# Transposing the first pair's raw queries, and asking for norms two row chunks earlier in the first batch

## The chip, the cores and the metric

The kernel runs on one core of one Trainium2 chip. The metric is the device time of one execution in microseconds (us), as the median over runs. The core has five engines with a queue of instructions each: TensorE (PE; its weight loads are shown apart as PEld), VectorE (DVE), ScalarE (ACT), GpSimd (POOL) and SyncE (SP), which here only issues transfers. Each queue runs in order, and an instruction at its head that waits for another engine or for a transfer holds up all that stand behind it.

## The reference

```python
# attention: q, k, v are (8, 12, 448, 64); everything is float32
def rmsnorm(x, g):
    return x / np.sqrt(np.mean(x * x, axis=-1, keepdims=True) + 1e-06) * g
scores = 1/np.sqrt(64) * rmsnorm(q, g_q) @ rmsnorm(k, g_k).transpose(0, 1, 3, 2)
scores = scores - scores.max(axis=-1, keepdims=True)
attn = np.exp(scores); attn = attn / (attn.sum(axis=-1, keepdims=True) + 1e-09)
x = (attn @ v).transpose(0, 2, 1, 3).reshape(8, 448, 768)
# spectral mixing and feed-forward
u = x + np.real(np.fft.fft(np.fft.fft(x, axis=1), axis=2))
un = (u - u.mean(-1, keepdims=True)) / np.sqrt(u.var(-1, keepdims=True) + 1e-06)
out = u + np.maximum(un @ w_ch1, 0) @ w_ch2     # w_ch1 (768, 3072), w_ch2 (3072, 768)
```

The weights are given in double precision, and the kernel converts them on the chip.

## The kernel before

The eight batches go through two programs. `aux(b)` does the attention of batch b and its spectral mixing; `ffn(b)` does the feed-forward part. `aux(0)` runs alone at the start, then `ffn(b)` is merged with `aux(b+1)`, which are both written as generators that yield an estimated cost. The opening stage, `aux(0)`, ends with the first matmul of `ffn(0)` (`up`, L1033), and nearly all of the span lies behind it.

Attention works through the 12 heads in six pairs, and a pair's 448 rows in four chunks of 112. For a pair, `load_pair` (L225) issues four loads on SP into the tile `raw` (two buffers): q for two heads, then k for two heads. Behind the first pair it calls `load_gains` (L197), four more loads on SP. `norm_pair` (L265) takes the mean squares: ACT squares q and k at once, DVE sums over 64 columns and applies 1/D and epsilon, POOL raises to the power -0.5 (`ss`), and q and k are multiplied by it into `qkn`, on DVE for the first two pairs, on POOL for the rest of the first two batches. `transpose_pair` (L309) loads and norms a pair, yields, lets PE turn q (`QT`), yields, then k (`KD`; ACT multiplies it on its way out of PSUM by `gneg`, the negative product of both gains and the scale), and yields. In the first batch the turned q goes through a PSUM bank of the tag S, of which there are two.

`softmax_pair` (L366) goes over the chunks: PE makes the scores of two heads (in S banks for chunks 0 and 2, in ffn banks for 1 and 3 of the first batch), DVE takes the minimum of each row (the scores carry a minus sign; `mn`), ACT takes the Exp with scale -1 and that minimum as bias, and sums. `value_pair` (L484) turns the results (`pt`, `rem`) and multiplies by v (`av`) one pair later. `attention` (L530) interleaves three generators: a pair's chunks, the values of the pair before and, from the second chunk on, the norm and the transposes of the next pair.

The program is recorded in this order and a scheduler then places instructions on the queues, so the order on an engine isn't quite that of the code; buffers are handed out in the order of the code. Conversions of weights (`convert`, L777: two steps on ACT, four on DVE, one on ACT, one on DVE for each block) are fed into the opening stage by the count n of yields: 0.12 of a block for each, fifteen blocks in all. At n = 40 the DFT tables are loaded, and from n = 112 to 126 a step of `aux(1)` runs for each yield. `warm` (L1096) gives PE eight matmuls on zeros at the very start. Instructions of DVE, ACT and POOL in the attention are recorded by one helper and so carry its line, L116.

Of the kernel before, what the change touches and what calls it, by code (L numbers as in the profile page):

```python
# [92 lines left out]
def spectral_block(ctx, tc, q, k, v, g_q, g_k, w1, w2, d1, d2, out, nb=B):  # L93
# [103 lines left out]
    def load_gains():  # L197
        for half in (lo, hi):
            nc.sync.dma_start(gneg[half], g_q.rearrange("(d o) -> d o", o=1))
            nc.sync.dma_start(gtmp[half], g_k.rearrange("(d o) -> d o", o=1))  # L200
        V.scalar_tensor_tensor(
            out=gneg, in0=gneg, scalar=-(D**-0.5), in1=gtmp, op0=ALU.mult, op1=ALU.mult
        )
# [20 lines left out]

    def load_pair(b, p):  # L225
        if b >= nb or (b, p) in loaded:
            return
        at = ORDERS[b > 0][p]
        raw = sb.tile([C, 2, 2, NC, D], F32, tag="raw", name=f"raw{b}_{p}")
        for i, src in enumerate((q, k)):  # L230
            for h in range(2):
                nc.sync.dma_start(
                    raw[:, i, h],
                    src[b, 2 * at + h].rearrange("(c t) d -> t c d", c=NC),
                )
        if b + p == 0:
            load_gains()
        loaded[b, p] = raw
        if not plain(b, p):
            load_values(b, p)  # L240
# [23 lines left out]

    def norm_pair(b, p):  # L265
        raw = loaded.pop((b, p))
        qk = sb.tile([C, 2, NC, 2, D], F32, tag="qk", name=f"qkn{b}_{p}", bufs=1)
# [10 lines left out]
        for i in range(2):  # L278
            (G if 2 <= nth < NPAIR * 2 else V).tensor_tensor(
# [29 lines left out]
    def transpose_pair(b, p):  # L309
# [8 lines left out]
        if plain_s(b, p):  # L318
            T = []
            for i, tag in enumerate(("QT", "KD")):  # L320
                pt = bank(QK_BANKS[b > 0][i], f"qk{b}_{p}_{i}")
                for c in range(NC):
                    nc.tensor.transpose(
                        pt[:, c * C : (c + 1) * C],
                        qk[:, i, c].rearrange("t h d -> t (h d)"),
                        ident[:C, :C],
                    )
# [38 lines left out]
    def softmax_pair(b, p, Pc):  # L366
# [3 lines left out]
        for c in range(NC):  # L370
# [31 lines left out]
            for h, s_ in enumerate(banks):  # L402
                V.tensor_reduce(mn[:, h : h + 1], s_, axis=AX.X, op=ALU.min)
                freed[tag] = A.activation(
# [4 lines left out]
                    scale=-1.0,  # L409
# [120 lines left out]
    def attention(b, xT, EO):  # L530
# [3 lines left out]
        for p in range(NPAIR):  # L534
# [4 lines left out]
            ahead = transpose_pair(*next_pair(b, p))  # L539
            for i in range(4):  # L540
                yield next(rows)
                for _ in range(2):
                    yield next(values, 0)
                if i >= 1:
                    yield next(ahead, 0)
# [550 lines left out]
    def warm():  # L1096
# [4 lines left out]
        for _ in range(8):  # L1101
# [52 lines left out]
```

## Time and profile before

| | us |
|---|---|
| median of 3 runs | 2117.45 (2114.3 to 2120.1) |
| the profiled execution, its own time | 2118.55 |
| span of its trace | 2116.8 |
| first matmul of the feed-forward part | at 172.06 |

The mean clock granted to PE over the span is 0.987 of full. In the trace's tables, each row starts with the time from the span's start and the duration. A bracket at a row's end gives the time for which the engine had been idle before, and what released it. Busy times are of single engines and overlap each other. "x2" means that two instructions of the same kind were merged into a row, whose duration is that of both.

### The profile page before, as it was taken

Reading aid. Unit: us, or ns where it says so; the run is one execution under the profiler, and the core shown is the slowest. Engines: PE = TensorE matmul, PEld = TensorE weight load, DVE = VectorE, ACT = ScalarE, POOL = GpSimd, SP = SyncE. Lnnn points to the kernel's source line nnn. Section 1 sums busy time; section 2 is a strip of 40 time slices with the busy share of each in tenths; the row PEclk is TensorE's granted clock in tenths of the full one; section 3 lists DMA queues with packets and bytes.
Section 4 is the critical chain, followed back from the end, with each engine's and each line's share of the span. In section 5 each row is a group of like instructions: output and inputs, shape, how many; then the busy total and the mean of one; then the engine's idle time right before and its main releaser. Section 6 shows DMA issues by size and latency. Waiting matters only on the chain.

```text
span 2116.8 us, 31277 instructions
## 1 busy us (share of the span) xinstructions
PE 2069.4 (98%) x11288; PEld 1813.9 (86%) x11288; DVE 1510.5 (71%) x2882; ACT 1109.8 (52%) x2436; POOL 195.1 (9%) x109
## 2 busy tenths in 40 slices
PE   7879999999999999999999999999999999999999
PEld 3346777999999999999999999999999999998998
DVE  6788999877875778667885778758786678743122
ACT  6878886555534666256652566436662465422100
POOL 3321110000100110000110011001000001000000
PEclk8998999999999999999999999999999999999999
DMA  7565979776556745576565855567555764459664
GB/s 228 172 178 202 309 244 298 243 225 181 168 183 202 223 150 177 178 239 183 172 188 171 247 167 170 185 196 221 173 164 178 235 196 150 153 172 291 196 217 152
DMA packets 294494, 422.12 MB, mean 199 GB/s; under 512 B 182994, under 2 KB 221315, under 8 KB 294340
## 3 DMA queue, kind: packets, MB, share of 16 engines
q1 hardware_dynamic: 293572, 419.43, 64.5%
q8 instruction: 90, 1.47, 0.3%
q10 hardware_dynamic: 768, 0.69, 0.1%
q14 instruction: 64, 0.52, 0.1%
HBM read 360.27 MB, written 65.28 MB: 201 GB/s over the span
## 4 chain that ended last, share of the span: by engine, by line
PE 90%; DVE 3%; ACT 2%; DMA 2%; issue 1%; SPq 1%; POOL 0%; DVEq 0%; ACTq 0%; POOLq 0%
PE h L1033 33%; PE o L1054 32%; PE S L399 6%; PE av L519 4%; PE pt L507 4%; PE y L650 2%; PE S L392 1%; PE qk L343 1%; PE x L682 1%; PE oT L966 1%; PE av L453 1%; PE rem L488 1%; DMA u_dram<-u 1%; PE un L911 1%; PE pt L445 1%
## 5 line engine op out<-in xcount | busy, mean ns | idle before, releaser
L1054 PE MATMUL o<-hs,w 128*128 128x448 f32 x3420 | 772.6, 370 | 2.6 <-DMA w<-w 2.5
L1033 PE MATMUL h<-unT,w 128*128 128x448 f32 x3402 | 765.9, 369 | 1.1 <-ACT unT L116 0.9
L1054 PEld LDWEIGHTS o<-hs,w 128*128 128x128 f32 x3420 | 632.3, 188 | 58.4 <-issue 7.7
L1033 PEld LDWEIGHTS h<-unT,w 128*128 128x128 f32 x3402 | 627.7, 188 | 55.1 <-issue 4.1
L116 ACT ACTIVATE P<-S,mn 112x448 f32<-112x448 f32 x384 | 243.7, 638 | 187.7 <-DVE mn L116 183.3
L116 DVE TENSOR_REDUCE mn<-S 112x1 f32<-112x448 f32 x384 | 234.4, 618 | 50.4 <-PE S L399 35.8
L116 ACT ACTIVATE hs<-h 128x448 fp32r<-128x448 f32 x192 | 104.3, 543 | 296.5 <-PE h L1033 295.3
L116 POOL TENSOR_TENSOR ss<-ss,nhalf 112x16 f32<-112x16 f32 x48 | 146.5, 3052 | 1123.8 <-DVE ss L116 1123.8
L116 DVE SCALAR_TENSOR_TENSOR hs<-h,hs 128x448 fp32r<-128x448 f32 x192 | 119.3, 621 | 147.1 <-ACT hs L116 145.8
L116 DVE TENSOR_TENSOR acc<-o,acc 128x448 f32<-128x448 f32 x240 | 148.4, 620 | 89.9 <-PE o L1054 88.4
L116 ACT CAST T<-pt 128x448 fp32r<-128x448 f32 x216 | 113.4, 531 | 94.2 <-PE pt L507 92.1
L116 DVE TENSOR_TENSOR T<-pt,T 128x448 fp32r<-128x448 f32 x216 | 132.5, 620 | 36.8 <-ACT T L116 35.3
L519 PE MATMUL av<-T,vhl 128*128 128x448 f32 x432 | 153.3, 385 | 0.0
L116 DVE TENSOR_SCALAR P<-P,sm 112x448 f32<-112x448 f32 x312 | 129.3, 452 | 4.9
L507 PE MATMUL pt<-ident,P 112*128 112x112 f32 x864 | 121.7, 259 | 0.0
L507 PEld LDWEIGHTS pt<-ident,P 112*128 112x128 f32 x864 | 102.8, 140 | 16.5
L399 PE MATMUL S<-KD,QT 128*112 128x448 f32 x288 | 110.0, 382 | 0.0
L399 PE MATMUL S<-rounded,QT 128*112 128x448 f32 x288 | 105.5, 366 | 0.0
L519 PEld LDWEIGHTS av<-T,vhl 128*128 128x128 f32 x432 | 80.7, 188 | 6.8
L392 PE MATMUL S<-KD,QT 64*112 64x448 f32 x192 | 64.2, 647 | 14.3 <-ACT KD L116 5.7
L116 POOL TENSOR_TENSOR rstd<-st,nhalf 112x1 f32<-112x1 f32 (+2 forms) x32 | 20.4, 636 | 608.7 <-DVE st L116 604.5
L116 ACT ACTIVATION_READ_ACCUMULATOR P<-S,mn 112x1 f32 x384 | 76.4, 199 | 0.0
(147 smaller groups left out, 2420.2 us busy)
## 6 DMA issues: line engine op xcount, KB each, us to landing
w<-w SPq DMA_DIRECT2D x285, 512.0 KB
w<-w SPq DMA_DIRECT2D x189, 768.0 KB
dblw<-w SPq DMA_DIRECT2D x30, 512.0 KB
dblw<-w SPq DMA_DIRECT2D x15, 768.0 KB
raw<-q SPq DMA_DIRECT2D x96, 112.0 KB
raw<-k SPq DMA_DIRECT2D x96, 112.0 KB
v<-v SPq DMA_DIRECT2D x96, 96.0 KB
u_dram<-u SPq DMA_DIRECT2D x24, 336.0 KB
```

The costliest lines, as they stand in the source:

```text
L116: ins = emit(*args, **kwargs)
L343: nc.tensor.transpose(pt[:, c * C : (c + 1) * C], qk[:, i, c].rearrange("t h d -> t (h d)"), ident[:C, :C],)
L392: mm = nc.tensor.matmul(s_, QT[hs, cs], KD[hs], start=True, stop=True)
L399: nc.tensor.matmul(s_, QT[:, h, cs], K[:, h], start=step == 0, stop=step == 1)
L445: nc.tensor.transpose(pt[:, c * C : (c + 1) * C], piece, ident[:C, :C])
L453: mm = nc.tensor.matmul(av[a, :S], v_[:, j, h], T[h], start=j == 0, stop=False)
L488: nc.tensor.transpose(rem[:, c * C : (c + 1) * C], Pc[c][:, 384:512], ident[:C, :C])
L507: nc.tensor.transpose(pt[:, c * C : (c + 1) * C], Pc[c][:, 512 * h + j * 128 : 512 * h + (j + 1) * 128], ident[:C, :C],)
L519: nc.tensor.matmul(av[:, :S], lv, T[:, i], start=(j == 0 and i == 0), stop=False)
L650: nc.tensor.matmul(o, src[:, par, t0 : t0 + n], D1[:, ri, par, cols], start=i != 1, stop=i != 0,)
L1033: pace(nc.tensor.matmul(o, w[:, a, c], unT[c][:, z], start=n == 0, stop=n == 17))
L1054: mm = nc.tensor.matmul(o, w[:, a, f], hs[4 * g + f][:, z], start=n == 0, stop=n == 11)
```

## The change

Five things are edited.

- The gain loads go to ACT's queue instead of SP's, and of the first pair k is loaded ahead of q.
- The first pair has its own norm, `norm_first`. k and q are squared, summed and raised to the power each on its own, k first. Only k is multiplied by its factors. q is left as loaded, stored chunk by chunk (`by_chunk`), and turned from the tile `raw`. Its factors are held in `scales` and come in later: each row minimum of the first pair's scores is multiplied by its factor, and the Exp takes the negated factor as its scale, one per row.
- The second pair's two products go from DVE to POOL.
- In the first batch, one step of the next pair's `transpose_pair` (its loads and norm) is taken ahead of the pair's four chunks. The transposes then follow chunks 1 and 2 instead of 2 and 3.
- Five warm-up matmuls instead of eight.

```diff
     def load_gains():
         for half in (lo, hi):
-            nc.sync.dma_start(gneg[half], g_q.rearrange("(d o) -> d o", o=1))
-            nc.sync.dma_start(gtmp[half], g_k.rearrange("(d o) -> d o", o=1))
+            nc.scalar.dma_start(gneg[half], g_q.rearrange("(d o) -> d o", o=1))
+            nc.scalar.dma_start(gtmp[half], g_k.rearrange("(d o) -> d o", o=1))
...
+    def by_chunk(x):
+        return x.rearrange("t h c d -> t (h c d)").rearrange(
+            "t (c h d) -> t h c d", c=NC, h=2
+        )
...
-        for i, src in enumerate((q, k)):
+        first = b + p == 0
+        for i, src in ((1, k), (0, q)) if first else ((0, q), (1, k)):
+            rows = by_chunk(raw[:, 0]) if first and i == 0 else raw[:, i]
             for h in range(2):
                 nc.sync.dma_start(
-                    raw[:, i, h],
+                    rows[:, h],
                     src[b, 2 * at + h].rearrange("(c t) d -> t c d", c=NC),
                 )
...
+    scales = cpool.tile([C, 2, 16], F32, name="scales")
+
+    def norm_first(raw):
+
+        part = [
+            slot("h", f"qkn0_0_{i}")[:C, : 2 * NC * D].rearrange(
+                "t (n d) -> t n d", d=D
+            )
+            for i in range(2)
+        ]
+        rows = raw.rearrange("t i h c d -> t i (h c) d")
+        for i in (1, 0):
+            A.activation(part[i], rows[:, i], AF.Square)
+            f = scales[:, i, :8]
+            V.tensor_reduce(f, part[i], axis=AX.X, op=ALU.add)
+            V.tensor_scalar(
+                out=f, in0=f, scalar1=1.0 / D, scalar2=EPS, op0=ALU.mult, op1=ALU.add
+            )
+            G.tensor_tensor(out=f, in0=f, in1=nhalf[:C, :8], op=ALU.pow)
+        V.tensor_tensor(
+            out=by_chunk(part[1].rearrange("t (h c) d -> t h c d", h=2)),
+            in0=raw[:, 1],
+            in1=scales[:, 1, :8]
+            .rearrange("t (h c) -> t h c", h=2)[:, :, :, None]
+            .broadcast_to([C, 2, NC, D]),
+            op=ALU.mult,
+        )
+        V.tensor_scalar(
+            out=scales[:, 0, 8:], in0=scales[:, 0, :8], scalar1=-1.0, scalar2=None,
+            op0=ALU.mult,
+        )
...
     def norm_pair(b, p):
         raw = loaded.pop((b, p))
+        if b + p == 0:
+            return norm_first(raw), None
...
-            (G if 2 <= nth < NPAIR * 2 else V).tensor_tensor(
+            (G if nth < NPAIR * 2 else V).tensor_tensor(
...
+                    rows = qk[i][:, c] if b + p == 0 else qk[:, i, c]
                     nc.tensor.transpose(
                         pt[:, c * C : (c + 1) * C],
-                        qk[:, i, c].rearrange("t h d -> t (h d)"),
+                        rows.rearrange("t h d -> t (h d)"),
...
                 V.tensor_reduce(mn[:, h : h + 1], s_, axis=AX.X, op=ALU.min)
+                scale = -1.0
+                if b + p == 0:
+                    n = 2 * c + h
+                    scale = scales[:, 0, 8 + n : 9 + n]
+                    V.tensor_tensor(
+                        out=mn[:, h : h + 1], in0=mn[:, h : h + 1],
+                        in1=scales[:, 0, n : n + 1], op=ALU.mult,
+                    )
...
-                    scale=-1.0,
+                    scale=scale,
...
             ahead = transpose_pair(*next_pair(b, p))
+            if b == 0:
+                yield next(ahead, 0)
             for i in range(4):
...
-        for _ in range(8):
+        for _ in range(5):
             nc.tensor.matmul(o, ident, w, start=True, stop=True)
```

What this does to the queues is shown at three places. The names in the rows are those of tiles: `ss_1`, `qkn_1` and `raw_1` belong to the second pair, `mn_0_2` and `S_0_2_1` to the first pair's chunk 2 (and its second head), and `_0` ahead of further numbers to the first pair. Line numbers before are those of the old kernel, after those of the new one.

The first is the start of DVE's queue, up to the first row minimum. Before:

```order
L1099 MEMSET warm 128x512
L116 TENSOR_REDUCE ss_0_144<-qkn_0_142 112x16
L116 SCALAR_TENSOR_TENSOR gneg<-gneg,gtmp 128x1
L116 TENSOR_SCALAR ss_0_144<-ss_0_144 112x16
L116 TENSOR_TENSOR qkn_0_142<-raw_0_115,ss_0_144 112x2x4x64 x2
L116 TENSOR_REDUCE ss_1_199<-qkn_1_197 112x16
L116 TENSOR_REDUCE mn_0_0_173<-S_0_0_0_174 112x1
```

After:

```order
L1156 MEMSET warm 128x512
L116 TENSOR_REDUCE scales<-qkn_0_1_141 112x8
L116 TENSOR_SCALAR scales<-scales 112x8
L116 SCALAR_TENSOR_TENSOR gneg<-gneg,gtmp 128x1
L116 TENSOR_REDUCE scales<-qkn_0_0_140 112x8
L116 TENSOR_SCALAR scales<-scales 112x8
L116 TENSOR_TENSOR qkn_0_1_141<-raw_0_116,scales 112x2x4x64
L116 TENSOR_SCALAR scales<-scales 112x8
L116 TENSOR_REDUCE ss_1_180<-qkn_1_178 112x16
L116 TENSOR_SCALAR ss_1_180<-ss_1_180 112x16
L116 TENSOR_REDUCE mn_0_0_188<-S_0_0_0_189 112x1
L116 TENSOR_TENSOR mn_0_0_188<-mn_0_0_188,scales 112x1
```

One product over k stands where two over q and k stood, and a small product follows the row minimum.

The second is the start of ACT's queue. Before:

```order
L116 ACT_TABLE_LOAD
L116 COPY flip<-ident 113x112
L116 COPY flip<-ident 113x1
L116 ACTIVATE qkn_0_142<-raw_0_115 112x1024
L116 COPY QT_0_155<-qk_0_0_150 128x448
L116 ACTIVATE KD_0_162<-qk_0_1_157,gneg 128x448
L116 ACTIVATE qkn_1_197<-raw_1_137 112x1024
```

After:

```order
L199 DMA gneg<-g_q 64x1
L200 DMA gtmp<-g_k 64x1
L116 ACT_TABLE_LOAD
L116 COPY flip<-ident 113x112
L116 COPY flip<-ident 113x1
L199 DMA gneg<-g_q 64x1
L116 ACTIVATE qkn_0_1_141<-raw_0_116 112x512
L200 DMA gtmp<-g_k 64x1
L116 ACTIVATE qkn_0_0_140<-raw_0_116 112x512
L116 ACTIVATE qkn_1_178<-raw_1_135 112x1024
L116 COPY QT_0_157<-qk_0_0_152 128x448
L116 ACTIVATE KD_0_164<-qk_0_1_159,gneg 128x448
```

The four gain loads have come in, two of them ahead of the table load, and the second pair is squared ahead of the first pair's copies out of PSUM.

The third is PE's queue from the first pair's chunk 1 to the second pair's first scores. Before:

```order
L392 MATMUL S_0_1_1_185<-KD_0_162,QT_0_155 112x448
L392 MATMUL S_0_2_0_220<-KD_0_162,QT_0_155 112x448
L392 MATMUL S_0_2_1_221<-KD_0_162,QT_0_155 112x448
L488 MATMUL rem_0_283<-ident,P_0_0_172 128x112
L445 MATMUL pt_0_0_0_293<-ident,P_0_0_172 128x112
L392 MATMUL S_0_3_0_237<-KD_0_162,QT_0_155 112x448
L445 MATMUL pt_0_0_0_293<-ident,P_0_1_182 128x112
L392 MATMUL S_0_3_1_238<-KD_0_162,QT_0_155 112x448
L488 MATMUL rem_0_283<-ident,P_0_1_182 128x112
L323 MATMUL qk_1_0_228<-ident,qkn_1_197 128x112 x4
```

After:

```order
L439 MATMUL S_0_1_1_202<-KD_0_164,QT_0_157 112x448
L370 MATMUL qk_1_0_224<-ident,qkn_1_178 128x112 x4
L543 MATMUL rem_0_306<-ident,P_0_0_187 128x112
L500 MATMUL pt_0_0_0_316<-ident,P_0_0_187 128x112
L439 MATMUL S_0_2_0_233<-KD_0_164,QT_0_157 112x448
L370 MATMUL qk_1_1_243<-ident,qkn_1_178 128x112 x4
L439 MATMUL S_0_3_0_252<-KD_0_164,QT_0_157 112x448
L500 MATMUL pt_0_0_0_316<-ident,P_0_1_199 128x112
L439 MATMUL S_0_3_1_253<-KD_0_164,QT_0_157 112x448
L543 MATMUL rem_0_306<-ident,P_0_1_199 128x112
L439 MATMUL S_0_2_1_234<-KD_0_164,QT_0_157 112x448
L439 MATMUL S_1_0_0_298<-KD_1_248,QT_1_229 112x448
```

The second pair's q transposes (`qk_1_0`) have moved ahead of all but chunks 0 and 1, and chunk 2's second head (`S_0_2_1`) has fallen behind chunk 3.

## Rows read from the trace of the kernel before

**Rows 1.** The page: busy time of each engine, share of the span, instructions.

```profile
PE 2069.4 (98%) x11288; PEld 1813.9 (86%) x11288; DVE 1510.5 (71%) x2882; ACT 1109.8 (52%) x2436; POOL 195.1 (9%) x109
```

**Rows 2.** Windows: us, busy PE, PEld, DVE, ACT, POOL, PEclk, DMA share, GB/s.

```profile
12.00:172.00 160.00, 126.09 (x645) 65.72 (x643) 126.48 (x234) 124.06 (x280) 44.09 (x26) 0.85 0.64 196
...
16.00:20.00 4.00, 0.84 (x6) 0.20 (x2) 4.00 (x10) 3.37 (x8) 2.65 (x1) 1.00 1.19 296
...
66.00:80.00 14.00, 11.10 (x63) 4.85 (x61) 7.38 (x16) 10.14 (x28) 5.52 (x3) 0.86 0.66 217
...
80.00:120.00 40.00, 34.06 (x202) 16.09 (x203) 38.23 (x66) 34.93 (x81) 13.06 (x6) 1.00 0.63 189
...
172.00:2116.00 1944.00, 1933.52 (x10628) 1743.99 (x10628) 1380.86 (x2642) 982.98 (x2154) 146.55 (x74) 1.00 0.65 200
```

**Rows 3.** Timeline, PE: the first matmul of the feed-forward part.

```profile
172.06 0.74 PE L1033 MATMUL h<-unT,w1e 128*128 128x448 f32 x1 [1.00 <-ACT unT L116]
```

**Rows 4.** Timeline, SP: start us, duration us, what is issued.

```profile
0.73 0.93 SPq L232 DMA_DIRECT2D raw<-q  x2
1.71 1.02 SPq L232 DMA_DIRECT2D raw<-k  x2
2.77 0.57 SPq L199 DMA_DIRECT2D gneg<-g_q  x1
...
5.29 1.12 SPq L232 DMA_DIRECT2D raw<-q  x2
```

**Rows 5.** Timeline, ACT: the start, and the first Exp.

```profile
0.74 1.28 ACT L116 ACT_TABLE_LOAD   x1 [0.74 <-PEq L1134]
2.17 0.38 ACT L116 COPY flip<-ident 113x112 f32<-113x112 f32 x2
4.93 1.06 ACT L116 ACTIVATE qkn<-raw 112x1024 f32<-112x1024 f32 x1 [2.38 <-DMA raw<-k]
...
16.63 0.63 ACT L116 ACTIVATE P<-S,mn 112x448 f32<-112x448 f32 x1 [1.82 <-DVE mn L116]
```

**Rows 6.** Timeline, DVE: the start, up to the first row minimum.

```profile
7.18 0.16 DVE L116 SCALAR_TENSOR_TENSOR gneg<-gneg,gtmp 128x1 f32<-128x1 f32 x1
7.27 0.17 DVE L116 TENSOR_SCALAR ss<-ss 112x16 f32<-112x16 f32 x1
10.56 1.29 DVE L116 TENSOR_TENSOR qkn<-raw,ss 112x512 f32<-112x512 f32 x2 [3.11 <-POOL ss L116]
14.85 1.22 DVE L116 TENSOR_REDUCE ss<-qkn 112x16 f32<-112x1024 f32 x1 [3.00 <-ACT qkn L116]
15.98 1.15 DVE L116 TENSOR_REDUCE mn<-S 112x1 f32<-112x448 f32 x2
```

**Rows 7.** Timeline, POOL: powers (ss, rstd) and products (qkn).

```profile
7.60 2.92 POOL L116 TENSOR_TENSOR ss<-ss,nhalf 112x16 f32<-112x16 f32 x1 [5.46 <-DVE ss L116]
...
70.63 2.04 POOL L116 TENSOR_TENSOR qkn<-raw,ss 112x512 f32<-112x512 f32 x2
...
103.34 3.48 POOL L116 TENSOR_TENSOR qkn<-raw,ss 112x512 f32<-112x512 f32 x2
...
164.18 0.55 POOL L116 TENSOR_TENSOR rstd<-st,nhalf 113x1 f32<-113x1 f32 x1 [14.69 <-DVE st L116]
```

**Rows 8.** Timeline, PE: a warm-up weight load, first scores, a late pair's transposes.

```profile
9.21 0.19 PEld L1102 LDWEIGHTS warmed<-warm,ident 128*128 128x128 f32 x1 [0.24 <-issue]
...
13.92 2.51 PE L392 MATMUL S<-KD,QT 64*112 64x448 f32 x12 [0.78 <-ACT KD L116]
...
72.73 0.60 PE L323 MATMUL qk<-ident,qkn 112*128 112x112 f32 x4 [2.02 <-POOL qkn L116]
```

**Rows 9.** Timeline, DVE: a wait for scores; one conversion step twice.

```profile
75.20 1.16 DVE L116 TENSOR_REDUCE mn<-S 112x1 f32<-112x448 f32 x2 [3.83 <-PE S L392]
...
104.35 1.58 DVE L806 CUSTOM_DVE_ANT_0 magw1e<-dblw1e,magw1e 128x1536 uint16<-128x1536 uint16 x1
...
111.64 0.95 DVE L806 CUSTOM_DVE_ANT_0 magw1e<-dblw1e,magw1e 128x1536 uint16<-128x1536 uint16 x1
```

More of the change, by code (lines that the diff above doesn't have):

```diff
@@ L229, in load_pair @@
         raw = sb.tile([C, 2, 2, NC, D], F32, tag="raw", name=f"raw{b}_{p}")
-        for i, src in enumerate((q, k)):
+        first = b + p == 0
+        for i, src in ((1, k), (0, q)) if first else ((0, q), (1, k)):
+            rows = by_chunk(raw[:, 0]) if first and i == 0 else raw[:, i]
             for h in range(2):
                 nc.sync.dma_start(
-                    raw[:, i, h],
+                    rows[:, h],
                     src[b, 2 * at + h].rearrange("(c t) d -> t c d", c=NC),
                 )
-        if b + p == 0:
+        if first:
             load_gains()
@@ L263, in next_pair @@
         return (b, p + 1) if p + 1 < NPAIR else (b + 1, 0)
+    scales = cpool.tile([C, 2, 16], F32, name="scales")
[27 more added lines that the diff above has]
+        )
+        turn = "t (c h d) -> t c h d"
+        return [
+            x.rearrange("t n d -> t (n d)").rearrange(turn, c=NC, h=2)
+            for x in (rows[:, 0], part[1])
+        ]
     def norm_pair(b, p):
         raw = loaded.pop((b, p))
+        if b + p == 0:
+            return norm_first(raw), None
         qk = sb.tile([C, 2, NC, 2, D], F32, tag="qk", name=f"qkn{b}_{p}", bufs=1)
```

## The prediction

> **What bounds the kernel now.** I read the busy times first [rows 1]: TensorE (PE) works 98% of the span, so only time in which it is not fed can be won. The table of windows [rows 2] shows where that is. From 172 us on PE is busy 1933.52 of 1944.00 us at full clock. In the opening stage, from 12 to 172 us, it is busy 126.09 of 160.00, and no other engine is full there either: VectorE (DVE) 126.48, ScalarE (ACT) 124.06. The stage is a relay between them, with DVE close to full in one part of it (38.23 of 40.00 us from 80 to 120). It ends with the first up matmul at 172.06 us [rows 3]. The change leaves the work ahead of that matmul alone but for a few instructions, and behind the first batch the order of all engines is as it was. So the question is by how much 172.06 moves; what follows moves with it one for one.
>
> **The start, step by step.** Today SP issues q, k, four gain loads, then the second pair [rows 4]. ACT squares q and k in one instruction at 4.93 us, 2.20 us after the last of the four issues ended at 2.73 [rows 4, 5]. DVE reduces (1.22), scales by 1/D, POOL takes the power (2.92), DVE multiplies twice (1.29 together, done at 11.85), PE transposes, and the first scores run at 13.92 [rows 6 to 8]. They are ready some 0.75 us later, but DVE has the second pair's reduction in front (14.85, 1.22), so the first row minimum starts at 15.98 and the first Exp at 16.63 [rows 5, 6].
>
> After the change k is loaded first. Its issues end at 0.73+0.93 = 1.66, so it lands at about 3.86 by the same 2.20. ACT is later than that: its queue now holds two gain loads ahead of the table load, and one each ahead of the two squares. On SP the four take 5.29-2.77 = 2.52, 0.63 each [rows 4]; at that price the table load moves from 0.74 to 2.00, the flip copies end at about 3.7, and the square of k runs from 4.3 to 4.85 (half of 1.06). Reduction to 5.5 (half of 1.22), power from 5.7. The last gain load is issued at 5.5 and lands at 7.7 by the same 2.20; the product of the gains stands in DVE's queue ahead of the reduction of q, so DVE is held until 7.7. Then reduction of q to 8.4, product of k (half of 1.29) to 9.15. In front of the k transposes PE has five warm-up calls instead of eight; the eleventh of today's sixteen weight loads for them starts at 9.21 [rows 8], so ten are out at about that time, and warm-up holds nothing. From the end of the product to the first scores is 13.92-11.85 = 2.07 today; so scores at about 11.2, ready at 12.0 at the latest, 11.5 if the q transposes are out before.
>
> The other branch is DVE's: ahead of the first minimum it has a negated copy of q's factors, which waits for the second power, and the second pair's reduction. A power on 8 columns isn't in the trace. It lies between 0.55 (1 column) and 2.92 (16 columns) [rows 7]; on the line between them it is 0.55+7/15*2.37 = 1.66. The second power starts at 8.5, ends at 10.2 (11.4 at the upper bound), the reduction follows to 11.4 (12.7). First minimum at 11.5 to 12.7, plus a small product of 0.09 ahead of each Exp: first Exp at 12.3 to 13.5 instead of 16.63. **Term one: -4.0 us**, between -3.1 and -4.4; I lean to the line between the two power rows, since the work is per column.
>
> **DVE's and POOL's work.** Of four products of 0.645, DVE keeps one: -1.94. It gets eight products on one column, one negation and one more 1/D step, ten small ones; the nearest rows are the 128x1 gains product at 7.18, behind which the next starts at 7.27, so 0.09 each and 0.16 at worst [rows 6]: +0.9 to +1.6. Net -1.0 to -0.3. DVE is full in a part of the stage alone, so **term two: -0.5**. POOL gets the second pair's two products, 2.04 instead of DVE's 1.29 [rows 7], and two powers for one; its queue is nearly empty there. An Exp with a scale per row instead of a constant I cost at nothing: it already reads one value per row as its bias. At worst it would add some 0.1 for each of eight, under ACT's idle time.
>
> **The norms asked for earlier.** Ahead of each pair's scores in the first batch one step more of the next pair runs: loads and norm before row chunk 0 and not after chunk 1, transposes of q after chunk 1 and of k after chunk 2. Squares, reductions, powers and raw loads move along, and SP, whose queue stands still while a raw load waits for a buffer that POOL's product has to free, gets to its weight loads earlier. What late norms cost today: at 70.63, behind a power, POOL starts products of 2.04, and PE, with transposes at the head of its queue, waits 2.02 to 72.73; behind it DVE waits 3.83 for scores [rows 7 to 9]. In 66 to 80 DVE is busy 7.38 of 14.00 [rows 2]. That is the one place where the norm alone is late: 0 to 3.83 to win. **Term three: -1.5**, less than half, because another wait comes in.
>
> That wait: for the first batch the transposed q takes one of the two S banks. Today it is asked for behind all scores of chunk 2; now it stands between chunk 1 and chunk 2. In PE's queue the second pair's q transposes stand ahead of the first pair's chunk 2, and the last scores of chunk 2 stand behind those of chunk 3, waiting for ACT's copy out of that bank. The same holds for each pair. Price: nothing if the norm is early, PE's 2.02 [rows 8] for each of five hand-overs if it is as late as at 72.73. **Term four: +1.0**, half of one such wait, since the norm starts two chunks earlier and its transposes one.
>
> The step counter that paces weight conversions and the look-ahead into the second batch runs by six steps more; all fifteen conversions and all fifteen look-ahead steps still fall into this stage, so that costs nothing.
>
> Sum: -4.0-0.5-1.5+1.0 = **-5.0 us**.
>
> **A rule weighed.** POOL's two products took 2.04 at 70.63 and 3.48 at 103.34, and while the latter ran, a conversion step of DVE took 1.58 at 104.35 against 0.95 at 111.64 [rows 7, 9]. So POOL and DVE hold each other up at times, and the change moves two products to POOL just when DVE converts the first weights. The Trainium skill (SBUF — State Buffer, Who interferes with whom) has a rule for this: a DVE instruction with two SBUF inputs and a GpSimd instruction that reads SBUF need the same port, and whoever comes second waits for the whole of the other. The trace agrees in kind. By that rule the second pair's norm would always be held up.
>
> **Rivals.** (1) *The lead is lost to transfers.* From 16 to 20 us the DMA engines are at 1.19 of what they can [rows 2], with four weight blocks and the third pair's rows under way. If these land no earlier, pair 2 starts when it does now, and terms one and three are gone. Against it: SP is 2.52 us earlier from its third issue on. Left: the DVE term and little else, -1.0, so 2116.5 us. (2) *The lead holds and the late norm goes entirely*, with no new wait: -4.4-1.0-3.8 = -9.2, so 2108.3 us. For it: DVE's 6.6 idle us between 66 and 80; against it: the bank. (3) *Slower: the S bank.* If q's transposes come late by as much as now, at five hand-overs, the price is 5*2.02 = 10.1, less term one: +6.1, so 2123.6 us. It decides from the point where the next pair's product on POOL ends over 4.0/5 = 0.8 us later, on the mean, than PE is ready for chunk 2. (4) *POOL held up* by DVE, always as at 103.34: 3.48-2.04 = 1.4 later at the second pair, when nothing else is queued to hide it: -3.6, so 2113.9 us. This is the rule of the page above. (5) That the change doesn't do what it says is excluded for the start, as the queues show; that norms are asked for earlier but run when they did is the forecast without its last two terms, -4.5.
>
> **How the numbers follow.** The profiled execution took 2118.55 us, 1.10 above the median of 2117.45. 2118.55-5.0 = 2113.55; against the median **2112.5 us**. The rivals' times are against the median too. Chances: forecast 0.40, rival 1 0.20, rival 2 0.27, rival 3 0.08, rival 4 0.05. What a measurement of this kernel can tell from no change is about 0.3%, 6.4 us. The forecast's own band is -2 to -8; a quarter of it lies beyond 6.4, so faster is 0.27+0.10 = 0.37. Slower is most of rival 3, 0.06; the rest, 0.57, is within. The range runs from somewhat below rival 2, 2105.5, to 2119.5, a little above no change; it leaves out rival 3 and the tails of the others.
>
> **What would show it.** In the changed profile: first Exp near 12.5 us (over 14 and term one is wrong); powers on 8 columns near 1.7; the first up matmul near 167 us; no wait of DVE for scores like the 3.83; PE's waits for POOL's products and for the copy of q out of the S bank short. If the first Exp is 4 us early and the up matmul isn't, rival 1 or 3 holds: then SP's queue and PE's waits tell which. A move of the time with 172.06 in place would make the whole account wrong.

## The result and the profile after

The changed kernel took 2134.92 us (2131.72 to 2141.3) beside 2118.01 us (2114.3 to 2120.1) of the kernel before: 1.0083 times as long, with a 95% interval of 1.0071 to 1.0095. That is slower, above the range on record and also above the slower rival. The profiled execution took 2131.72 us, its span 2129.9, at a mean granted clock of 0.982 (before 0.987).

The page's first part, busy time of each engine:

```profile
PE 2081.3 (98%) x11282; PEld 1817.8 (85%) x11282; DVE 1517.1 (71%) x2890; ACT 1112.9 (52%) x2437; POOL 202.5 (10%) x112
```

The windows of after that answer to [rows 2]:

```profile
12.00:172.00 160.00, 131.66 (x610) 65.55 (x607) 126.38 (x225) 117.18 (x262) 51.01 (x25) 0.82 0.62 185
...
66.00:80.00 14.00, 12.60 (x74) 5.98 (x72) 12.12 (x19) 13.69 (x31) 3.73 (x3) 1.00 0.79 234
80.00:120.00 40.00, 34.21 (x166) 16.65 (x167) 31.87 (x58) 29.58 (x74) 15.14 (x6) 0.83 0.61 189
...
172.00:2129.00 1957.00, 1940.61 (x10652) 1747.99 (x10650) 1386.25 (x2656) 990.63 (x2167) 145.78 (x76) 1.00 0.65 199
```

PE is busier in the opening stage than before (131.66 against 126.09) and does less: 610 matmuls against 645. ACT has lost 7 us of work. The first 200 us say it in one row for each kernel, before first, then after:

```profile
0.00:200.00 200.00, 163.84 (x806) 92.24 (x807) 156.40 (x286) 153.34 (x335) 49.05 (x36) 0.87 0.62 188
```

```profile
0.00:200.00 200.00, 163.12 (x743) 85.93 (x744) 154.39 (x282) 148.31 (x323) 58.45 (x39) 0.84 0.60 179
```

PE's busy time is the same within 0.7 us, but 63 matmuls fewer are done, at a lower clock. From 172 us on a matmul takes 1933.52/10628 = 0.182 us [rows 2], so what is left over costs 63*0.182 = 11.5 of the 13.1 us by which the span grew. The opening stage itself ends 7.6 us later; this is the timeline's row that answers to [rows 3]:

```profile
179.67 0.47 PE L1090 MATMUL h<-unT,w1e 128*128 128x448 f32 x1 [2.90 <-ACT unT L116]
```

Up to that matmul PE does the same work in both kernels but for six warm-up matmuls. Windows that end there, before first, then after:

```profile
0.00:172.06 172.06, 135.90 (x661) 69.94 (x661) 129.71 (x241) 126.84 (x284) 48.64 (x36) 0.86 0.64 193
```

```profile
0.00:179.67 179.67, 145.24 (x655) 72.64 (x655) 134.82 (x249) 128.81 (x286) 58.45 (x39) 0.83 0.62 184
```

PE is idle for 36.2 us of the stage before and for 34.4 after, so all of the 7.6 us, and 1.7 more, is longer busy time, as the profile counts it. The waits shown below came in place of others.

The start went as forecast. POOL, then ACT, then DVE, from the start to 18 us (the powers are `scales` and `ss`; L844 to L863 are steps of a weight conversion):

```profile
5.48 1.66 POOL L116 TENSOR_TENSOR scales<-scales,nhalf 112x8 f32<-112x8 f32 x1 [3.35 <-DVE scales L116]
7.91 2.06 POOL L116 TENSOR_TENSOR scales<-scales,nhalf 112x8 f32<-112x8 f32 x1 [0.77 <-DVE scales L116]
...
14.55 2.88 POOL L116 TENSOR_TENSOR qkn<-raw,ss 112x512 f32<-112x512 f32 x2
```

```profile
12.72 0.72 ACT L116 ACTIVATE P<-S,mn,scales 112x448 f32<-112x448 f32 x1 [1.95 <-DVE mn L116]
...
13.44 0.88 ACT L844 ACTIVATE magw1e<-dblw1e 128x768 f32<-128x768 f32 x1
14.21 0.91 ACT L846 ACTIVATE dblw1e<-dblw1e 128x768 uint32<-128x768 uint32 x1
14.99 0.73 ACT L116 ACTIVATE P<-S,mn,scales 112x448 f32<-112x448 f32 x1
```

```profile
15.06 1.00 DVE L116 TENSOR_TENSOR mn<-mn,scales 112x1 f32<-112x1 f32 x1
...
16.56 1.68 DVE L859 SCALAR_TENSOR_TENSOR magw1e<-dblw1e,magw1e 128x768 uint32<-128x768 uint32 x1
```

The first Exp runs at 12.72 instead of 16.63. But behind it ACT does the first weight block's two steps, and the second Exp comes only at 14.99. DVE's steps of the same block run beside POOL's product for the second pair, and both take longer than elsewhere. PE has that product at the head of its queue. PE's timeline, the first scores and the waits for a product (`qkn`):

```profile
10.82 1.76 PE L439 MATMUL S<-KD,QT 64*112 64x448 f32 x8 [0.78 <-ACT KD L116]
16.10 0.60 PE L370 MATMUL qk<-ident,qkn 112*128 112x112 f32 x4 [3.51 <-POOL qkn L116]
...
34.42 1.01 PE L370 MATMUL qk<-ident,qkn 112*128 112x112 f32 x4 [0.39 <-POOL qkn L116]
...
50.83 0.60 PE L370 MATMUL qk<-ident,qkn 112*128 112x112 f32 x4 [2.66 <-POOL qkn L116]
...
68.24 0.60 PE L370 MATMUL qk<-ident,qkn 112*128 112x112 f32 x4 [0.83 <-POOL qkn L116]
...
86.93 1.01 PE L370 MATMUL qk<-ident,qkn 112*128 112x112 f32 x4 [2.45 <-POOL qkn L116]
```

Five waits, 9.84 us together. Windows of after at the first wait and behind it (columns as in [rows 2], the clock third from the end):

```profile
12.00:20.00 8.00, 4.49 (x18) 1.96 (x14) 7.57 (x14) 5.89 (x13) 5.35 (x3) 0.85 1.16 274
20.00:30.00 10.00, 9.63 (x20) 2.77 (x19) 6.17 (x13) 7.53 (x17) 0.18 (x1) 0.50 0.71 184
30.00:40.00 10.00, 9.22 (x39) 4.83 (x40) 9.42 (x13) 7.70 (x16) 5.61 (x3) 0.60 0.75 228
```

PE is at the lower of its levels (1.2 GHz) all through 20 to 30 us and for most of the ten after that. In the kernel before it is there for much of the same time too: 0.60 from 20 to 30 us, 0.50 in the ten after. So the trace alone names a suspect, the early transposes, but not what made the product late, nor what it cost.

### The profile page after: what moved, and what is told of

Read it like the earlier page. It is cut to its first block, busy times and chain, and to the rows that moved or that the text cites. A ratio compares the mean times of both kernels' runs of the same rounds, so it can differ in the third digit from the quotient of the medians.

```text
span 2129.9 us, 31159 instructions
## 1 busy us (share of the span) xinstructions
PE 2081.3 (98%) x11282; PEld 1817.8 (85%) x11282; DVE 1517.1 (71%) x2890; ACT 1112.9 (52%) x2437; POOL 202.5 (10%) x112
## 4 chain that ended last, share of the span: by engine, by line
PE 91%; DVE 4%; DMA 2%; ACT 2%; issue 1%; POOL 1%; SPq 0%; POOLq 0%; DVEq 0%; ACTq 0%
PE h L1090 32%; PE o L1111 32%; PE S L446 6%; PE av L574 4%; PE pt L562 4%; PE S L439 2%; PE y L707 2%; PE qk L390 1%; PE av L508 1%; PE x L739 1%; PE oT L1023 1%; PE un L968 1%; PE rem L543 1%; PE pt L500 1%; PE ab L795 1%
## 5 line engine op out<-in xcount | busy, mean ns | idle before, releaser
L116 ACT ACTIVATE P<-S,mn 112x448 f32<-112x448 f32 x376 | 238.9, 638 | 192.9 <-DVE mn L116 183.5
L439 PE MATMUL S<-KD,QT 64*112 64x448 f32 x192 | 74.3, 663 | 4.7 <-ACT P L116 3.8
```

What stands on the lines that cost most here:

```text
L116: ins = emit(*args, **kwargs)
L439: mm = nc.tensor.matmul(s_, QT[hs, cs], KD[hs], start=True, stop=True)
```

## The experiments

All runs were timed beside the kernel before on the same chip, 2117.2 to 2119.1 us. Times are medians, ratios are to that kernel, with 95% intervals; the two can differ by some 2 us, and differences of that size aren't read.

| run | what it is | us | ratio |
|---|---|---|---|
| e1_start | start alone, second pair's products on DVE | 2116.0 | 0.9982 (0.9973 to 0.9992) |
| e4_no_early | start, products on POOL | 2115.5 | 0.9990 (0.9981 to 0.9999) |
| e2_early | before + early step | 2124.9 | 1.0032 (1.0021 to 1.0044) |
| e3_dve2 | changed, products on DVE | 2124.9 | 1.0029 (1.0017 to 1.0041) |
| e7_bank | changed, q not through an S bank | 2133.3 | 1.0067 (1.0054 to 1.0080) |
| c1_count | before + six bare yields | 2138.5 | 1.0105 (1.0089 to 1.0121) |
| f1_shift | c1, look-ahead moved back | 2118.4 | 0.9997 (0.9986 to 1.0009) |
| c2_norm | before + norm early | 2116.1 | 0.9995 (0.9985 to 1.0005) |
| c3_turn | before + norm and transposes early | 2127.0 | 1.0048 (1.0034 to 1.0062) |
| e6_no_count | changed, step not counted | 2119.9 | 1.0006 (0.9995 to 1.0016) |
| d1_old_turn | changed, transposes at the old place | 2134.7 | 1.0078 (1.0063 to 1.0093) |
| d2_old_turn_nc | both | 2117.9 | 0.9998 (0.9988 to 1.0008) |
| g1_shift | changed, look-ahead moved back | 2132.9 | 1.0062 (1.0050 to 1.0074) |
| g2_unfed | changed, early steps feed no conversion | 2119.7 | 1.0005 (0.9996 to 1.0015) |
| g3_unfed1 | the same at the first pair alone | 2121.8 | 1.0017 (1.0009 to 1.0026) |
| h2_old_shift | d1, look-ahead moved back | 2123.9 | 1.0026 (1.0014 to 1.0038) |
| g4_best | e4, look-ahead six steps later | 2130.0 | 1.0053 (1.0040 to 1.0065) |
| h1_conv_late | e4, conversions four steps later | 2119.8 | 1.0002 (0.9993 to 1.0010) |

**The parts apart.** The first theory, W, was that the early step makes PE wait at its queue's head; rivals were P (the second pair's products on POOL), S (the new start) and C (the step counter).

The start alone:

```diff
-            if b == 0:
-                yield next(ahead, 0)
...
-            (G if nth < NPAIR * 2 else V).tensor_tensor(
+            (G if 2 <= nth < NPAIR * 2 else V).tensor_tensor(
```

> The new start alone: k first, gain loads on ACT, the first pair's own norm, five warm-up calls; the second pair's products on DVE and the norms at their old place. Theory W (the wait): the loss of the changed kernel comes from the early request, which puts the next pair's transposes ahead of chunk 2's scores at the head of PE's queue, where PE waits for POOL. Then this kernel keeps the 4 us lead of the first Exp: about 2114 us (2110 to 2117), PE's waits for POOL's products near the 2.8 us of before. Theory S (the start itself upsets what follows): 2122 us or more.

2116.0 us: S falls; the start gains, 2 us by the medians, 4 by the ratio. The early step alone, in the kernel before:

```diff
             ahead = transpose_pair(*next_pair(b, p))
+            if b == 0:
+                yield next(ahead, 0)
```

> The kernel before with the early request alone (one step of the next pair ahead of the four chunks, counted as a step); start and products as before. Theory W: the whole loss and no lead from the start, about 2132 us (2126 to 2140), PE waits for POOL's products near 10 us in total. Theory P (the second pair's products on POOL are the cause): 2118 us. Theory S: 2118 us.

2124.9: it costs about 7 us without any of the rest. The changed kernel with the second half of the first diff alone:

> The changed kernel with the second pair's two products back on DVE. Theory W: the first of PE's waits for POOL's products (3.5 us at 16 us) shrinks to the power's share, the later ones stay: 2130 us (2125 to 2136). Theory P: the loss is gone, 2113 us or so.

2124.9: the products on POOL are worth 10 us of the loss. But the first wait hardly shrinks: PE now waits for the same product from DVE, which itself waited for POOL's power.

```profile
15.31 1.20 PE L370 MATMUL qk<-ident,qkn 112*128 112x112 f32 x8 [3.27 <-DVE qkn L116]
```

The first half of that diff alone, with the products on POOL:

> The changed kernel without the early step; the second pair's products stay on POOL. So far the start alone gave 2116.0 and taking the products of the second pair back to DVE brought the changed kernel from 2134.9 to 2124.9 us. If these products cost by themselves, whatever the place of the transposes (theory P): about 2116+10 = 2126 us. If they cost because PE now has the second pair's transposes in front of the first pair's chunks 2 and 3 (theory I, an interaction): 2114 to 2118.5 us, with no wait of PE for this product of over 1 us in the first 30 us.

2115.5: on POOL they cost nothing, as long as nothing is asked for early. P by itself falls; products and early step hurt together. The S bank, which the prediction's slower rival blamed:

```diff
-QK_BANKS = (("S", "either"), ("q", "q"))
+QK_BANKS = (("q", "q"), ("q", "q"))
```

> The changed kernel with the first batch's turned q and k both going through the q bank and none through an S bank, so that chunk 2's scores need not wait for the next pair's transposes. Theory W in its bank form: most of the loss goes, 2118 us or less. If the transposes stand at the head of PE's queue whatever their bank, or the loss has to do with the step count (theory C: six steps more shift conversions and look-ahead), it stays near 2135 us.

2133.3, within 2 us of the changed kernel: freeing the S bank doesn't help. The run isn't a clean test, since it trades waits: PE's waits for POOL's products are 5.4 us together up to 180 us (changed kernel 10.6), those of the scores for `KD` 6.6 (changed kernel 0.8). The run without counted steps, below, keeps the bank and is the better test.

**The early step apart.** It does three things: it asks for the norm early (N), moves the transposes ahead of chunk 2 (T), and counts a step more for each pair (C). In the kernel before, one each. The counter, behind the line `ahead = ...`:

```diff
+            if b == 0:
+                yield 0
```

> The kernel before with a bare yield ahead of each pair of the first batch: the step counter runs by six more and nothing else is asked for earlier. The early step alone cost 2124.85-2118.2 = 6.7 us. Theory C (the counter: weight conversions and the look-ahead come at other places): most of that, 2122 to 2126 us. Theory T (the transposes' place in PE's queue) and theory N (the norm's work ahead of chunk 0): 2118.2 within 1.5 us, as the prediction had the counter cost nothing.

2138.5, more than the whole change. The norm:

```diff
+            if b == 0:
+                next(ahead, 0)
...
-                    yield next(ahead, 0)
+                    yield 0 if b == 0 and i == 1 else next(ahead, 0)
```

> The kernel before with only the norm asked for early: the next pair's loads and norm are recorded ahead of chunk 0, the transposes of q and k keep their places behind chunks 2 and 3, and the step counter runs as before. Theory N (squares, reductions, powers and products of the norm get in the way of the present pair's chunks): 2121 to 2126 us. Theories C and T: 2118 us or, since the norm is then done two chunks before PE wants it, down to 2115 us.

2116.1: nothing that can be told from no change. Norm and transposes, with the first two lines of that diff alone:

> The kernel before with the norm asked for early and the transposes behind chunks 1 and 2 as in the changed kernel, but with the early step not counted, so that the step counter runs as before. Theory T (PE's queue has the transposes ahead of chunks 2 and 3 and waits there): 2123 to 2127 us, and the run with the norm alone near 2118. Theory C: 2117 to 2119 us. Theory N: as the run with the norm alone.

2127.0: without the new start the transposes' place does cost, 11 us over the norm alone. PE's longest wait there, of the timeline:

```profile
52.08 1.01 PE L323 MATMUL qk<-ident,qkn 112*128 112x112 f32 x4 [4.84 <-POOL qkn L116]
```

**The same in the changed kernel.** First the counter out, transposes early (the step is `next(ahead, 0)` without its yield):

> The changed kernel with the early step not counted; the transposes stay behind chunks 1 and 2. Theory T: no better than the changed kernel, 2130 to 2140 us (without the start, the turn alone gave 2127.0 uncounted and 2124.9 counted, so the counter gave a little back there). Theory C: 2114 to 2120 us.

2119.9: 15 of the 17 us are gone, with the transposes and the bank where the change has them. T, my theory at that point, falls for the changed kernel. The transposes back, counter in (the second part of the norm's diff):

> The changed kernel with the norm still asked for early and the early step still counted, but with the transposes behind chunks 2 and 3 as before. Theory T (PE's queue has the transposes ahead of chunks 2 and 3 and waits there; the counter does harm only by chance): 2114 to 2119 us. Theory C (a counter that runs by six more costs what it cost alone, 2138.45-2117.2 = 21 us, as long as the transposes have their old place): 2130 to 2140 us.

2134.7: no better than the changed kernel. Both:

> The changed kernel with the norm asked for early, the transposes behind chunks 2 and 3 and the step counter as before. If the turn and the counter are all that hurts (T and C): 2112 to 2117 us, like the start with POOL's products (2115.5) and the norm alone (2116.1). If something else of the changed kernel hurts as well, over 2120 us.

2117.9. So in the changed kernel the transposes' place is worth some 2 us, a size that isn't read as a difference, and the counter 15 to 17.

**What the counter paces.** It feeds weight conversions (K) and sets where the look-ahead into the second batch stands (L); at n = 40 it also has the DFT tables loaded. In the kernel with bare yields the look-ahead was moved back to the same work:

```diff
-AHEAD_FROM = 112
-AHEAD_UNTIL = 127
+AHEAD_FROM = 118
+AHEAD_UNTIL = 133
```

> The kernel before with the bare yields of the counter run, but with the stretch in which the look-ahead into the second batch runs moved from 112 to 126 to 118 to 132, so that it stands at the same work as before. If the counter's 21 us come from the look-ahead standing six steps earlier: 2117 to 2121 us. If they come from the weight conversions, which each yield feeds by 0.12 of a block: still 2132 to 2140 us.

2118.4: there it is the look-ahead, all of it; the DFT tables are still loaded six steps early. Windows of c1_count, then of f1_shift:

```profile
120.00:180.00 60.00, 39.40 (x203) 27.25 (x198) 42.75 (x88) 37.14 (x76) 12.46 (x10) 0.77 0.46 143
```

```profile
120.00:180.00 60.00, 47.08 (x263) 32.33 (x260) 52.32 (x110) 45.91 (x98) 13.86 (x10) 0.89 0.46 144
```

With the look-ahead six steps early PE does 203 matmuls in this stretch, else 263. What it waits for stands in the timelines, c1_count first (the scores are the second batch's, and the first batch's transforms stand behind them):

```profile
149.14 1.01 PE L392 MATMUL S<-KD,QT 64*112 64x448 f32 x4 [3.37 <-ACT P L116]
153.16 1.84 PE L392 MATMUL S<-KD,QT 64*112 64x448 f32 x4 [3.01 <-ACT P L116]
```

```profile
137.00 1.01 PE L392 MATMUL S<-KD,QT 64*112 64x448 f32 x4 [1.27 <-ACT P L116]
...
169.99 1.01 PE L392 MATMUL S<-KD,QT 64*112 64x448 f32 x4 [2.71 <-ACT P L116]
```

But that is the smaller part. The opening stage of c1_count ends at 175.16 (first up matmul), only 3.1 us later than in the kernel before, and up to 200 us it lags f1_shift by 40 matmuls (788 against 828), some 7 us at 0.182 each. The rest comes where `ffn(0)` runs with `aux(1)`. A landmark there is the last turn of `un`, the normalized input of the second batch's feed-forward part, c1_count first, then f1_shift:

```profile
449.55 0.56 PE L913 MATMUL un<-ident,un 113*128 113x113 f32 x4
```

```profile
426.51 0.56 PE L913 MATMUL un<-ident,un 113*128 113x113 f32 x4
```

They are 23.0 us apart; the same landmark of the first batch is 5.3 apart (177.59 and 172.25). Which wait costs this isn't shown.

The same move in the changed kernel:

> The changed kernel with the look-ahead moved from steps 112 to 126 to steps 118 to 132, so that it stands at the same work as before; the conversions are still fed by the early steps. The changed kernel took 2134.9 us, with nothing counted 2119.9. Theory L (the look-ahead's place, as with the bare yields): 2117 to 2123 us. Theory K (the weight conversions come earlier among the first pairs' chunks): 2131 to 2136 us. Half each would be some 2127.

2132.9: here only 2 us, 4 by the ratios. The trace shows two effects that nearly cancel. The first up matmul comes at 176.22, 3.5 us earlier than in the changed kernel, but the second batch's landmark comes later, changed kernel first, then g1_shift:

```profile
438.82 0.95 PE L968 MATMUL un<-ident,un 113*128 113x113 f32 x8
```

```profile
440.72 0.95 PE L968 MATMUL un<-ident,un 113*128 113x113 f32 x8
```

The other branch, counted steps that feed no conversion:

```diff
-                yield next(ahead, 0)
+                next(ahead, 0)
+                yield -1
...
-    for n, _ in enumerate(aux(0)):
+    for n, cost in enumerate(aux(0)):
...
-        if n:
+        if n and cost >= 0:
             convert_some(CONVERT_EARLY)
```

> The changed kernel with the early steps counted, but without the 0.12 of a conversion that each of them feeds; the look-ahead stays six steps early. Theory K: 2117 to 2123 us. Theory L: 2131 to 2136 us.

2119.7: K, all that the counter costs, though the look-ahead and the load of the DFT tables stay six steps early here. And with `yield -1 if p == 0 else 0`, at the first pair alone:

> As the one before, but only the first pair's early step feeds no conversion; the other five do. In the changed kernel's trace ACT does the first block's two steps ahead of the second Exp, DVE's steps hold up POOL's product for the second pair, and PE waits 3.51 us for it; with nothing counted that wait is gone. If this first wait is what theory K pays for: 2122 to 2127 us, as when the product went back to DVE (2124.9). If the later pairs' conversions pay, or theory L holds: 2131 to 2136 us.

2121.8: one step's 0.12 of a block, fed ahead of the first pair, is worth 13 of the 17 us. The feed adds up, so without it every later conversion comes a step later too, and this run can't tell the first pair's share from theirs. What it moves at the first pair is seen in e6_no_count, ACT, then POOL, then PE:

```profile
13.08 0.72 ACT L116 ACTIVATE P<-S,mn,scales 112x448 f32<-112x448 f32 x1 [1.94 <-DVE mn L116]
...
13.81 0.72 ACT L116 ACTIVATE P<-S,mn,scales 112x448 f32<-112x448 f32 x1
...
14.52 0.90 ACT L844 ACTIVATE magw1e<-dblw1e 128x768 f32<-128x768 f32 x1
```

```profile
14.02 2.04 POOL L116 TENSOR_TENSOR qkn<-raw,ss 112x512 f32<-112x512 f32 x2
```

```profile
14.68 0.32 PE L543 MATMUL rem<-ident,P 112*128 112x112 f32 x1 [1.73 <-ACT P L116]
...
15.12 0.60 PE L370 MATMUL qk<-ident,qkn 112*128 112x112 f32 x4
```

The second Exp is ahead of the block's steps, the product takes 2.04 instead of 2.88, and PE turns the second pair at 15.12 with no wait for it. In g3_unfed1 ACT has the same order, and the wait is 1.18:

```profile
16.08 0.60 PE L370 MATMUL qk<-ident,qkn 112*128 112x112 f32 x4 [1.18 <-POOL qkn L116]
```

That this first wait is what the 13 us pay for was my theory, and the traces don't bear it out. In g3_unfed1 PE has waited 1.73 us for the first Exp just before, so it turns the second pair at 16.08, beside 16.10 in the changed kernel. In e3_dve2, 10 us faster than the changed kernel, it waits 3.27. In g1_shift, 11 us slower than g3_unfed1, the product takes 2.36 as in g3_unfed1, and PE turns the pair at 15.35.

Nor does the lead run through from the first pair. DVE inverts the sums of the six pairs (RECIPROCAL `sums`, start in us) at:

| | pair 1 | 2 | 3 | 4 | 5 | 6 |
|---|---|---|---|---|---|---|
| changed kernel | 33.38 | 46.09 | 65.22 | 87.88 | 107.03 | 121.00 |
| g3_unfed1 | 30.65 | 48.71 | 69.26 | 83.99 | 102.15 | 113.22 |
| g2_unfed | 30.13 | 52.38 | 67.96 | 85.09 | 103.06 | 118.03 |
| e6_no_count | 26.96 | 46.13 | 61.00 | 77.16 | 99.55 | 110.00 |

g3_unfed1 and g2_unfed are ahead of the changed kernel at the first pair, behind at the second and third, and ahead from the fourth on. The rows of the last pair, changed kernel first, then g3_unfed1:

```profile
121.00 0.20 DVE L116 RECIPROCAL sums<-sums 112x8 f32<-112x8 f32 x1
```

```profile
113.22 0.20 DVE L116 RECIPROCAL sums<-sums 112x8 f32<-112x8 f32 x1 [0.81 <-ACT sums L116]
```

By the first up matmul (173.76 in g3_unfed1, 179.67 in the changed kernel) PE has been idle for 27.4 us in g3_unfed1 and 34.4 in the changed kernel. So in these two traces the feed costs PE some 7 us of waits, but which ones, behind the first pair, isn't shown.

The clock differs as well, in one trace. Windows of e6_no_count:

```profile
12.00:20.00 8.00, 6.24 (x26) 2.51 (x22) 7.57 (x15) 5.93 (x13) 3.98 (x3) 1.00 1.09 275
20.00:30.00 10.00, 9.30 (x19) 3.36 (x18) 8.60 (x19) 9.81 (x24) 4.20 (x2) 0.59 0.63 159
30.00:40.00 10.00, 8.38 (x52) 4.79 (x52) 7.64 (x10) 8.17 (x15) 1.33 (x2) 0.90 1.04 333
```

In these 28 us PE does 97 matmuls here, 77 in the changed kernel. But the execution that was traced is the fastest of twelve of e6_no_count (2113.85 us, median 2119.87). g2_unfed and g3_unfed1 do 81 in the same time, at a clock of 0.50 from 20 to 30 us as in the changed kernel:

```profile
20.00:30.00 10.00, 8.75 (x17) 3.07 (x16) 6.48 (x15) 6.49 (x13) 0.98 (x1) 0.50 0.63 160
```

That row is g3_unfed1's. So the clock of these 28 us isn't where the 13 us come from.

**What stayed.** The kernel with the old place of the transposes (d1) had the same order on ACT, and like c1_count it is late behind the opening stage: its second batch's landmark comes at 446.21, against 438.82 in the changed kernel. With the look-ahead moved back:

> The changed kernel with the transposes behind chunks 2 and 3, the early step counted (2134.7 us), and the look-ahead moved back by six steps. If the look-ahead's place is the loss there, as with the bare yields (2138.5, and 2118.4 when moved back): 2116 to 2122 us. If it is the first block's conversion ahead of the second Exp, as in the changed kernel: 2130 to 2136 us.

2123.9, between the two: the look-ahead is most of it there, and the landmark comes at 428.21 (428.10 in the kernel before). Two tries for a faster kernel, both from e4_no_early. The look-ahead later than today, by the diff of f1_shift:

> The changed kernel without the early step at all (2115.5 us) and with the look-ahead moved to steps 118 to 132, six later than in the kernel before. If an earlier look-ahead costs because its scores stand at the head of PE's queue ahead of the first batch's own work, a later one could give some more: 2105 to 2113 us. If less of it then fits into the opening stage: 2117 to 2125 us.

2130.0: six steps late cost 14 us, as six steps early cost 20. Again most of it is lost behind the opening stage: against e4_no_early the first batch's landmark is 1.4 us late (171.46 and 170.04), the second's 20.1 (442.95 and 422.83). Conversions begun later, with `if n > 4:` for `if n:`:

> The changed kernel without the early step (2115.5 us), with the feed of weight conversions begun four steps later. One step earlier among the first pair's chunks cost the changed kernel 13 us. If the later feed keeps the first block's steps out of the way of the first pair's Exps: 2108 to 2113 us. If the place today is already clear of them, or the conversions then crowd later pairs: 2115 to 2122 us.

2119.8, no gain. The fastest of all are e1_start and e4_no_early, both ahead of the two kernels compared, by 0.1 to 0.2% of the kernel before.

## Why the prediction was wrong

**The step that failed** is one sentence: that six more steps of the counter cost nothing, since all conversions and look-ahead steps still fall into the stage. They do, but the question was beside which work, not in which stage. Counting the steps costs 15 us (2134.9 beside 2119.9 uncounted), and the conversions that they feed account for all of it (g2_unfed, 2119.7). With the counter's conversions taken out (g2_unfed) the kernel is at 1.0005 of the kernel before; the range on record ends at 2119.5/2117.45 = 1.0010. The rows of ACT's queue that were shown with the change end a few entries ahead of the place: there the first block's two conversion steps stand between the first two Exps. By what chain of waits the early feed costs its 15 us stays open: that the wait at 16.10 is what is paid for, as I had it, the traces don't bear out.

A second sentence failed too: that what follows moves with 172.06 one for one. In the traces that matmul moved by 7.6 us and the span by 13.1; in c1_count by 3.1 and the span by 18.5.

**Term one** had the right mechanism and the right size at its own place: first Exp at 12.72 (forecast 12.3 to 13.5), powers on 8 columns 1.66 and 2.06 (1.66). At the end the start alone gives 0.9982 (0.9973 to 0.9992), that is 1.7 to 5.7 us, which holds the 4.0; with the products on POOL it is 0.2 to 4.0. The term stands, at its size or half of it.

**Term two.** The product on POOL is worth nothing either way alone (e1 beside e4). With the early step it costs 10 us, not the 1.4 of rival 4 (e3_dve2). "Its queue is nearly empty there" is true, but the product took 2.88 while DVE's steps of the conversion ran beside it, and 2.04 in e6_no_count. The Trainium skill (SBUF — State Buffer, Who interferes with whom) has DVE instructions with two SBUF inputs and GpSimd instructions that read SBUF share a port. The trace agrees in kind: DVE's L859, with two inputs, took 1.68 beside the product, a product on one column 1.00 (0.16 elsewhere in that trace). That this is rival 4's mechanism at a higher price isn't shown: with the products on DVE PE still waits 3.27. An Exp with a scale per row took 0.73 us on the mean, one with a constant 0.65: 0.08 for each of eight, near the 0.1 that the prediction had at worst.

**Term three.** The norm early alone can't be told from no change (c2_norm, 0.9995, 0.9985 to 1.0005): the interval holds the 1.5 us and nothing as well. The wait of 3.83 that it was to remove [rows 9] has given way to others, DVE's for scores at 54.35 and 111.18:

```profile
54.35 0.62 DVE L116 TENSOR_REDUCE mn<-S 112x1 f32<-112x448 f32 x1 [3.41 <-PE S L439]
...
111.18 0.62 DVE L116 TENSOR_REDUCE mn<-S 112x1 f32<-112x448 f32 x1 [3.35 <-PE S L439]
```

**Term four and rival 3.** The rival priced five waits for a late product at 5*2.02 = 10.1 us, and the trace has them: 9.84 us, 1.97 on the mean, well past its point of 0.8. I gave it 0.08 since the norm starts two chunks earlier. It named the wrong reason, though: with the steps not counted, 15 of the 17 us are gone with the S bank used as before (e6_no_count). Without the counted steps the transposes' place costs some 2 us in the changed kernel (e6 beside d2), which doesn't contradict term four's +1.0; in the kernel before it costs 11 (c3 beside c2). Why the new start makes that difference isn't shown.

**What the account left out** is PE's clock and the stage behind. It summed PE's waits, but in the changed kernel PE was idle 1.7 us less ahead of the first up matmul than before and busy 9.3 us longer with the same work, at a mean clock of 0.83 instead of 0.86. The clock's part isn't measured by itself. And c1_count, d1_old_turn, g1_shift and g4_best lose most behind the opening stage, where the prediction expected nothing to change.

## What to carry to other kernels

A counter that paces several things is a hidden argument of every edit that adds a step: find what is read off it, and look on each engine's queue at what has moved beside what, not only whether the totals still fit. When work is asked for earlier, keep the pacing where it was (here by not counting the step), and tune the two apart. Don't carry a price from one kernel to another either: the same product on POOL cost nothing in one and 10 us in the other. And follow a loss by landmarks from stage to stage before naming a wait: the longest wait in view wasn't shown to be the one that is paid for.

## What the runs showed that was not expected

- Six steps of the look-ahead, forward or back, cost 20 and 14 us (c1_count beside f1_shift, g4_best beside e4_no_early), about as much as any other edit here, and most of it behind the stage in which the steps stand: 23.0 and 20.1 us at the second batch's landmark, 5.3 and 1.4 at the first's. What runs short there isn't shown.
- A power on 8 columns took 1.66 us once and 2.06 once, on 16 columns 2.92 [rows 7]: less than half and more than half.
- PE's clock fell to its lower level in e6_no_count too, between 20 and 30 us, though from 12 us on no wait of PE for another engine had been longer than 1.73 us. In the changed kernel it fell already between 16 and 18 us (in windows of 2 us), right behind the wait of 3.51; but in g2_unfed it fell in the same two microseconds (0.69), with no wait over 1.73 since 12 us.
